# A two-layer decode block on one core: the last MLP block written out on its own

## The chip, the cores and the metric

One core of a Trainium2 chip runs the whole kernel. TensorE (PE) multiplies matrices out of SBUF into PSUM, VectorE (DVE) and ScalarE (ACT) work on SBUF and PSUM, GpSimd (POOL) on SBUF, and SyncE (SP) issues the DMA transfers between HBM and SBUF. Each engine works through its own instructions in order; they are ordered against each other by semaphores. The metric is device time in microseconds (us), less is better. The kernel before takes 1168.49 us, the median of 3 runs (1168.44 to 1168.51).

## What is computed

Eight sequences decode one token each. Attention over a cache of 8192 positions (32 query heads, 8 key heads, 128 wide) and an MLP (512 to 1792 to 512, SiLU) alternate, twice, with the same weights and the same cache both times:

```python
def _layernorm(x, axis=-1, eps=1e-5):
    m = jnp.mean(x, axis=axis, keepdims=True)
    v = jnp.var(x, axis=axis, keepdims=True)
    return (x - m) / jnp.sqrt(v + eps)
...
    def _B_ref(x, w1, w2):
        h = jnp.einsum("bsd,df->bsf", x, w1)
        h = _silu(h)
        out = jnp.einsum("bsf,fd->bsd", h, w2)
        return out

    x = A_x
    x = x + _A_ref(_layernorm(x, axis=-1), A_k_cache, A_v_cache, A_wq, A_wo)
    x = x + _B_ref(_layernorm(x, axis=-1), B_w1, B_w2)
    x = x + _A_ref(_layernorm(x, axis=-1), A_k_cache, A_v_cache, A_wq, A_wo)
    x = x + _B_ref(_layernorm(x, axis=-1), B_w1, B_w2)
    return x
```

x is (8, 1, 512) in bf16; the two caches have 128 MiB each. `_A_ref` is x@wq, softmax of the scaled scores, times V, and @wo.

## The kernel before, in words

**Tasks and steps.** A task is one attention over one (layer, sequence, key head): 2 x 8 x 8 = 128 tasks, in the order that `make_tasks` gives, and 8 steps to a task, so 1024 steps (NG). The main loop runs over the steps, p, and at each emits what is due there: key transposes (`emit_t_until`, VectorE, L487), scores (`emit_s`, TensorE, L553), the softmax of the task before in its phases (row maximum at phase 0, L564 and L566, then a GpSimd all-reduce, shift, exp on ScalarE at L580, and so on), P times V 14 steps behind the scores (`emit_pv`, L617), a copy and a fold of the result (L629, L634; the fold is a pair of fp32 matmuls), its scaling into the transposed activations (L646), and a head's part of the wo product (`add_heads`, L751). What is emitted earlier stands earlier in the queue of its engine.

**Loads.** Keys and values come in granules of 512 KB into the 28 slots of one SBUF area, `ARENA`. `plan_loads` sorts them by the step that needs them, picks a slot for each and notes the step behind which it may be issued; `issue_until(p)` issues those that are due, all on SyncE's queue. Part of the keys stays in its slots from the first layer to the second (`wide` loads). In the plan the last 28 loads go to 28 different slots: the first of them is the third granule of keys of sequence 7, head 0, into slot 20, which the scores of step 1005 read; the last is a granule of values.

**Ordering.** `op` and `mm_group` name what they read and write; `Sync.acquire` turns that into semaphore waits, leaves out what the engine has waited for already, and for TensorE leaves out waits on itself. VectorE and ScalarE do wait for their own earlier results.

**The last block.** Behind the loop the remaining heads are added up, and `block_stages` (L774) with n = 8 does residual, LayerNorm, MLP and residual for all eight sequences, the activations lying transposed as [128, 4, 8] (feature in the partition, four groups of 128, sequence). The same function with n = 1 does the first layer's block for one sequence at a time, inside the main loop. For n = 8:
- the residual: one VectorE add from the PSUM bank `MISC` (L763);
- `ln_stages` (L649): a reduce over the four groups (L686), an all-reduce over the partitions on GpSimd (L688), subtract (L694), square on ScalarE (L700), reduce (L701), all-reduce (L703), then the inverse root on VectorE, from a bit-shift seed by three Newton rounds (L708 to L718), and the product into `xnT` (L720). With n = 1 it goes by Ln and Exp on ScalarE instead (L669, L671) and one correcting step;
- w1: 56 matmuls into `MISC` (`project`, L733); SiLU as exp of the negative on ScalarE (L783), add 1, reciprocal, multiply on VectorE (L787 to L789), over 112 columns;
- w2: 56 matmuls into `MISC` (L733); the second residual (L763);
- four identity matmuls back to [8, 512] (L933), one VectorE copy to SBUF as bf16 (L940), one store (L942).

`SCp` are the two PSUM banks of the scores, `QSp` that of the expanded queries, `E` an fp32 SBUF tile which `P` and `Xr` view as bf16.

Of the kernel before, what the change touches and what calls it, by code (L numbers as in the profile page):

```python
# [8 lines left out]
LN_EPS = 1e-5  # L9
# [3 lines left out]
GUESS = 0.5 ** (1.0 / 3.0)  # L13

GRP = 8
GPT = 8
GPG = 2
NSLOT = 28
# [9 lines left out]
NSCP = 2  # L28
# [11 lines left out]
NAT = 2  # L40
CW = 32
SETTLE = 1

BF16 = mybir.dt.bfloat16
# [194 lines left out]
def _build(ctx, nc, A_x, A_k_cache, A_v_cache, A_wq, A_wo, B_w1, B_w2, out):  # L239
    B, _sq, D = A_x.shape  # L240
# [36 lines left out]
    ARENA = sb([128, NSLOT * SLOT], BF16, "arena")  # L277
# [67 lines left out]
    syn = Sync(nc, ctx)  # L345
# [6 lines left out]
    def res(name):  # L352
        if name not in R:
            R[name] = Res(name)
        return R[name]

    def r_half(slot, h):
        return res(f"slot{slot}_{h}")

    def op(eng, inst_fn, reads=(), writes=()):  # L360
        reads = [res(n) if isinstance(n, str) else n for n in reads]
        writes = [res(n) if isinstance(n, str) else n for n in writes]
        syn.acquire(eng, reads, writes)
        inst = inst_fn()
        tok = syn.mark(inst, eng)
        syn.release(tok, reads, writes)
        return tok
# [38 lines left out]
    with nc.Block() as block:  # L406

        @block.sync
        def _(sync_eng):
# [9 lines left out]
                reads=["ident"], writes=["ident"],  # L419
# [6 lines left out]
                reads=["ident"], writes=["hm"],  # L426
# [5 lines left out]
                reads=["ident"], writes=["own_x"],  # L432
# [3 lines left out]
            for n in range(NSCP):  # L436
# [11 lines left out]
               reads=["own_x", "hm"], writes=["sel"])  # L448
# [322 lines left out]

            settle = [idle] * SETTLE

            def block_stages(xs, rxs, n, fine=False):  # L774

                x0, x1, x2 = xs
                r0, r1, r2 = rxs
                p1, p2 = PIECES[:2] if fine else (1, 1)

                ev, re = (tiny["eh"], "eh") if n == 1 else (E[:, 0:FT * n], "P")  # L780

                def expo():
                    op(act, lambda: act.activation(ev, MISC[:, 0:FT * n], ACT.Exp, scale=-1.0),  # L783
                       reads=["MISC"], writes=[re])

                def silu():
                    op(dve, lambda: dve.tensor_scalar(ev, ev, 1.0, None, op0=ALU.add), reads=[re], writes=[re])  # L787
                    op(dve, lambda: dve.reciprocal(ev, ev), reads=[re], writes=[re])
                    op(dve, lambda: dve.tensor_tensor(hsT[:, 0:FT * n], MISC[:, 0:FT * n], ev, ALU.mult),  # L789
                       reads=["MISC", re], writes=["hsT"])  # L790

                def attended():
                    add_residual(x1, r1, x0, r0, n, CW if n == 1 else n)

                st = along([attended], ln_stages(x1, r1, n)) + settle
                st += joined(project(w1_sb, "w1", FT, KT, lambda k: xnT[:, k, 0:n], "xnT", n, p1), expo)
                st += [silu, idle]
                return st + joined(
                    project(w2_sb, "w2", KT, FT, lambda k: hsT[:, k * n:(k + 1) * n], "hsT", n, p2),
                    lambda: add_residual(x2, r2, x1, r1, n, n))  # L800

            def along(stages, more):
                return stages[:-1] + joined(stages[-1:], more[0]) + more[1:]
# [29 lines left out]
            def add_heads(b):  # L833
# [6 lines left out]
                else:  # L840
# [6 lines left out]
                        start=True, stop=True,  # L847
# [15 lines left out]

            emit_q(0)

            chain = []
            chain_b = [None]
            turn = [0]
# [11 lines left out]
            for p in range(NG + LP + GPT + FOLD + 1):  # L880
                tq = (p + LQ) // GPT
                if (p + LQ) % GPT == 0 and tq < ntask:
                    layer, b, _g = tasks[tq]
                    if layer == 1 and chain and chain_b[0] == b:
                        while chain:
                            chain.pop(0)()
                    emit_q(tq)
                emit_t_until(p + LT)
                if p % GPG == GPG - 1 and p < NG:
                    emit_s(p)  # L890
                if (p - LP) % GPG == GPG - 1 and 0 <= p - LP < NG:
                    emit_pv(p - LP)
                copied = p - LP - GPT
                if copied >= 0 and copied % GPT == 0 and copied // GPT < ntask:
                    emit_own(copied // GPT)
                folded = p - LP - GPT - FOLD_AT
                if folded >= 0 and folded % GPT == 0 and folded // GPT < ntask:
                    emit_fold(folded // GPT)
                ti, ph = p // GPT - 1, p % GPT
                if 0 <= ti < ntask and ph in soft:  # L900
                    for f in soft[ph]:
                        f(ti)
                if chain:
# [27 lines left out]
            mm_group(  # L931
                [
                    lambda kt=kt: pe.matmul(  # L933
                        MISC[0:B, kt * 128:(kt + 1) * 128], XT[0][:, kt, :], ident[:, :], start=True, stop=True,
                    )
                    for kt in range(KT)
                ],
                reads=["XT0", "ident"], writes=["MISC"],
            )
            op(dve, lambda: dve.tensor_copy(Xr[0:B, :], MISC[0:B, :]), reads=["MISC"], writes=["P"])  # L940
            syn.acquire(sp, reads=[res("P")])
            sp.dma_start(out_v, Xr[0:B, :]).then_inc(osem, 16)  # L942
            sp.wait_ge(osem, 16)

# [27 lines left out]
```

## Time and profile before

| | |
|---|---|
| median of 3 runs | 1168.49 us |
| the profiled execution | 1168.66 us |
| its span, first to last instruction | 1166.9 us |
| PE busy | 745.6 us (64%) |
| DVE busy | 628.2 us (54%) |
| ACT busy | 322.1 us (28%) |
| POOL busy | 117.9 us (10%) |
| moved by DMA | 467.10 MB, mean 400 GB/s |
| last transfer of values landed | 1150.6 us |
| last block's first residual starts | 1153.61 us |
| store issued | 1165.22 us |

Times in a profile run from the start of the span. A page has the busy share of each engine in 40 equal slices (a digit is tenths), the clock that TensorE was granted (PEclk, tenths), the chain of waits that ended last, and groups of instructions: line, engine, operation, output<-inputs, shape and count, then busy us and mean ns of one, then the engine's idle time ahead of them and what ended it. The timeline lists instructions as start, length, instruction, and in brackets the idle time of that engine before it and what it waited for. PEld is TensorE's weight load, which overlaps PE.

### The profile page before, as it was taken

The numbers are of one execution on the slowest core, as the hardware profiler recorded it, in microseconds if no ns is written. First come the engines' busy times: TensorE is split into PE (matmuls) and PEld (weight loads), VectorE is DVE, ScalarE is ACT, GpSimd is POOL, SyncE is SP. The second block draws the span as 40 slices with busy tenths as digits, with TensorE's granted clock in tenths as the row PEclk, the third lists the DMA queues.
The fourth block names the chain that finished last, engine by engine and source line by source line (L and its number), as shares of the span: only waits on it lengthen the run. The fifth ranks groups of instructions, "written<-read, shape, count | busy, mean of one in ns | idle before, by whom it ended". The sixth has DMA issues, their size and how long they took to land.

```text
span 1166.9 us, 31181 instructions
## 1 busy us (share of the span) xinstructions
PE 745.6 (64%) x13304; PEld 409.7 (35%) x13304; DVE 628.2 (54%) x1403; ACT 322.1 (28%) x756; POOL 117.9 (10%) x298
## 2 busy tenths in 40 slices
PE   1436676666756686567756676568766675567775
PEld 1213343234422353234423343235323442234333
DVE  3726662666446653656356553666266644566362
ACT  0202224223322224222413233223422233223331
POOL 0000011001100111001100110001100010001100
PEclk9755567655765568555765586655765577557755
DMA  9999999999999999999999999999999999999993
GB/s 363 395 396 411 408 403 412 417 410 402 403 418 413 408 391 414 415 409 407 407 415 411 403 393 415 416 408 407 410 417 409 400 398 420 411 408 407 408 408 143
DMA packets 116587, 467.10 MB, mean 400 GB/s; under 512 B 12240, under 2 KB 18144, under 8 KB 108768
## 3 DMA queue, kind: packets, MB, share of 16 engines
q1 hardware_dynamic: 116448, 465.11, 99.6%
q8 instruction: 104, 1.70, 0.6%
q14 instruction: 35, 0.29, 0.1%
HBM read 465.05 MB, written 0.01 MB: 399 GB/s over the span
## 4 chain that ended last, share of the span: by engine, by line
DMA 58%; SPq 22%; PE 12%; issue 4%; DVE 2%; ACT 0%; POOL 0%; POOLq 0%; DVEq 0%; ACTq 0%
DMA arena<-in_A_v_cache_dram 50%; SPq L374 22%; DMA arena<-in_A_k_cache_dram 8%; PE OTp L617 4%; PE SCp L553 3%; PE MISC L733 3%; PE OTp L634 2%; DVE arena L487 1%; PE TPp L598 1%; DVE row L564 0%; SPq L100 0%; PE MISC L751 0%; PE QSp L514 0%; POOL tops L569 0%; POOL ssa L589 0%
## 5 line engine op out<-in xcount | busy, mean ns | idle before, releaser
L487 DVE STREAM_TRANSPOSE arena<-arena 128x1024 int32<-128x1024 int32 x352 | 435.8, 1239 | 276.1 <-DMA arena<-in_A_k_cache_dram 276.0
L617 PE MATMUL OTp<-arena,PT 128*8 128x256 bf16 x4096 | 276.4, 365 | 364.5 <-DMA arena<-in_A_v_cache_dram 350.9
L580 ACT ACTIVATE E<-SCp,row 128x512 bf16<-128x512 f32 x128 | 181.1, 1415 | 489.0 <-DVE row L576 414.3
L553 PE MATMUL SCp<-arena,QB 128*16 128x128 bf16 (+2 forms) x4608 | 243.3, 354 | 11.1 <-DVE row L609 2.8
L617 PEld LDWEIGHTS OTp<-arena,PT 128*8 128x8 bf16 x4096 | 63.1, 86 | 509.3 <-DMA arena<-in_A_v_cache_dram 487.0
L553 PEld LDWEIGHTS SCp<-arena,QB 128*16 128x16 bf16 x4608 | 103.8, 108 | 69.6 <-issue 30.9
L634 PEld LDWEIGHTS OTp<-sel,E 128*128 128x128 f32 x512 | 103.6, 283 | 44.8 <-issue 32.8
L602 ACT COPY PT<-TPp 128x256 bf16<-128x256 bf16 x128 | 47.7, 373 | 252.0 <-PE TPp L598 252.0
L634 PE MATMUL OTp<-sel,E 128*128 128x4 f32 x512 | 114.7, 329 | 1.3 <-issue 0.8
L569 POOL PARTITION_ALL_REDUCE tops<-top x128 | 47.7, 373 | 549.0 <-DVE top L566 543.5
L589 POOL PARTITION_ALL_REDUCE ssa<-ssm x128 | 56.1, 438 | 384.8 <-ACT ssm L587 384.8
L564 DVE TENSOR_REDUCE row<-SCp 128x1 f32<-128x512 f32 x128 | 84.9, 663 | 11.9 <-PE SCp L553 11.8
L598 PE MATMUL TPp<-ident,E 128*128 128x128 bf16 x512 | 69.4, 281 | 3.7 <-ACT E L580 3.6
L609 DVE RECIPROCAL row<-ssa 128x4 f32<-128x4 f32 x128 | 18.7, 146 | 75.1 <-POOL ssa L589 75.1
L598 PEld LDWEIGHTS TPp<-ident,E 128*128 128x128 bf16 x512 | 39.3, 120 | 51.3 <-issue 31.6
L629 ACT COPY E<-OTp 128x256 f32<-128x256 f32 x128 | 48.2, 376 | 3.8 <-PE OTp L617 3.8
L733 PE MATMUL MISC<-xnT,wq 128*128 128x32 bf16 (+1 forms) x1152 | 35.6, 185 | 15.4 <-DVE xnT L720 14.3
L733 PEld LDWEIGHTS MISC<-xnT,wq 128*128 128x128 bf16 x1152 | 34.2, 104 | 21.9 <-issue 21.0
L751 PEld LDWEIGHTS MISC<-at,wo 128*128 128x128 bf16 x1024 | 33.1, 106 | 22.4 <-DVE row L576 10.1
L527 DVE TENSOR_TENSOR QB<-QSp,row 128x64 bf16<-128x64 f32 x128 | 25.8, 202 | 25.4 <-PE QSp L514 25.3
L587 ACT ACTIVATE ssm<-row 128x4 f32<-128x4 f32 x128 | 37.9, 296 | 3.9
L751 PE MATMUL MISC<-at,wo 128*128 128x32 bf16 x1024 | 37.5, 188 | 1.0 <-DVE row L573 0.4
(72 smaller groups left out, 278.9 us busy)
## 6 DMA issues: line engine op xcount, KB each, us to landing
arena<-in_A_v_cache_dram SPq DMA_DIRECT2D x512, 512.0 KB, 11.0
arena<-in_A_k_cache_dram SPq DMA_DIRECT2D x192, 512.0 KB, 8.2
arena<-in_A_k_cache_dram SPq DMA_DIRECT2D x24, 2048.0 KB, 22.4
arena<-in_A_k_cache_dram SPq DMA_DIRECT2D x32, 1024.0 KB, 20.3
wq<-in_A_wq_dram SPq DMA_DIRECT2D x1, 4096.0 KB, 16.3
wo<-in_A_wo_dram SPq DMA_DIRECT2D x1, 4096.0 KB, 34.7
w<-in_B_w_dram SPq DMA_DIRECT2D x2, 1792.0 KB, 27.1
E<-in_A_x_dram SPq DMA_DIRECT2D x1, 8.0 KB
```

The lines of the kernel that those rows point to most:

```text
L374: eng.dma_start(out_ap, in_ap).then_inc(counter.sem, 16)
L487: op(dve, lambda: dve.transpose(words, words), reads=[r_half(slot, 0), r_half(slot, 1)], writes=[r_half(slot, 0), r_half(slot, 1)])
L553: lambda n=n, t=t: pe.matmul(SCp[bank][t * QUAD:t * QUAD + USED, lo * 128:(lo + len(slots)) * 128], QB[qn][:, n, :], keys(t, n), start=(n ...
L564: op(dve, lambda: dve.tensor_reduce(rowmax[:, :], SCp[bank][:, :], AX.X, ALU.max), reads=[f"SC{bank}"], writes=["rowmax"])
L580: op(act, lambda: act.activation(P[:, :].rearrange("p (x j k) -> p k x j", x=CPB, k=NGRAN), SCp[bank][:, :].rearrange("p (k x j) -> p k x ...
L589: op(pool, lambda: pool.partition_all_reduce(ssa[st][:, :], ssm[st][:, :], 128, bass.bass_isa.ReduceOp.add), reads=[f"ssm{st}"], writes=[f ...
L598: lambda c=c: pe.transpose(tpv[:, c, :], P[:, c * 128:(c + 1) * 128], ident[:, :])
L617: lambda t=t, y=y: pe.matmul(OTp[ob][t * QUAD:t * QUAD + XW * REP, 0:XW * DH], PT[pb][:, k, t, y * XW:(y + 1) * XW].rearrange("p x r -> p ...
L629: op(act, lambda: act.copy(E[:, :], OTp[ob][:, 0:XW * DH]), reads=[f"OT{ob}"], writes=["P"])
L634: lambda x=x: pe.matmul(OTp[ob][:, 0:REP], E[:, x * DH:(x + 1) * DH], sel[:, x, :], start=(x == 0), stop=(x == XW - 1))
L733: lambda o=o, k=k: pe.matmul(MISC[:, o * n:o * n + w], w_sb[:, k, o * 128:(o + 1) * 128], rhs_of(k).to_broadcast([128, w]) if n == 1 else ...
L751: lambda o=o, h=h: pe.matmul(MISC[:, o * w:(o + 1) * w], wo_sb[:, h, o * 128:(o + 1) * 128], rhs_of(h).to_broadcast([128, w]) if n == 1 el ...
```

## The change

The last block no longer goes through `block_stages`. A function of its own, `last_block`, replaces it and what followed; `block_stages` with n = 1 and the main loop stay, but for one call.
- `last_constants`, called at the end of step NG - GPT = 1016, fills two 128x128 matrices with 1/512, one bf16 and one fp32, in the slot whose last load comes first in the plan. That slot's remaining space takes the block's small fp32 tiles.
- LayerNorm: four bf16 matmuls against the first matrix leave the mean of each sequence in every partition of `QSp`; VectorE subtracts, squares and reduces over the groups; one fp32 matmul against the second matrix leaves the variance. ScalarE takes Ln and Exp(-0.5 ...) with the constants of the n = 1 path, and VectorE one correcting round in three steps.
- The MLP in two halves of 7 x 128 hidden features. w1 of each half goes into its own bank of `SCp`; exp, add, reciprocal and multiply follow per half on 56 columns; w2 runs the first half's hidden features for all outputs and then the second's, adding up in `MISC`.
- The result: two identity matmuls into each bank of `SCp`, one half copied out by VectorE, the other by ScalarE; the store waits for both.

```diff
+            calm_slot = min(range(NSLOT), key=lambda n: max(d.slot <= n < d.slot + d.wide and i for i, d in enumerate(loads)))
+            r_calm = [r_half(calm_slot, h) for h in range(2)]
+            spare = ARENA[:, calm_slot * SLOT:(calm_slot + 1) * SLOT]
...
+            def last_constants():
+                op(dve, lambda: dve.memset(mean_w, 1.0 / D), writes=r_calm + ["mean_w"])
+                op(dve, lambda: dve.memset(var_w, 1.0 / D), reads=r_calm, writes=["var_w"])
+
+            def last_block():
...
+                mm_group([
+                    lambda k=k: pe.matmul(QSp[:, 0:B], mean_w, x1[:, k, :], start=(k == 0), stop=(k == KT - 1))
+                    for k in range(KT)
+                ], reads=["mean_w", "XT1"], writes=["QS"])
...
+                op(dve, lambda: dve.tensor_tensor(
+                    c3, x1[:, :, :], QSp[:, 0:B].unsqueeze(1).to_broadcast(wide), ALU.subtract),
+                   reads=["XT1", "QS"], writes=["c32"])
+                op(dve, lambda: dve.tensor_tensor(q32, c32, c32, ALU.mult), reads=["c32"], writes=["q32"])
+                op(dve, lambda: dve.tensor_reduce(part, q3.rearrange("p k b -> p b k"), AX.X, ALU.add),
+                   reads=["q32"], writes=["part"])
+                mm_group([lambda: pe.matmul(QSp[:, B:2 * B], var_w, part, start=True, stop=True)],
+                         reads=["var_w", "part"], writes=["QS"])
+                var = QSp[:, B:2 * B]
+                op(act, lambda: act.activation(gain, var, ACT.Ln, bias=eps[:, 0:1], scale=GUESS ** -2),
+                   reads=["QS", "eps"], writes=["gain"])
+                op(act, lambda: act.activation(gain, gain, ACT.Exp, scale=-0.5), reads=["gain"], writes=["gain"])
+                op(dve, lambda: dve.tensor_tensor(step_, gain, gain, ALU.mult), reads=["gain"], writes=["step_"])
+                op(dve, lambda: dve.scalar_tensor_tensor(step_, var, LN_EPS, step_, op0=ALU.add, op1=ALU.mult),
+                   reads=["QS", "step_"], writes=["step_"])
+                op(dve, lambda: dve.scalar_tensor_tensor(gain, step_, 3.0 * GUESS ** 2, gain, op0=ALU.subtract, op1=ALU.mult, reverse0=True),
+                   reads=["step_", "gain"], writes=["gain"])
+                op(dve, lambda: dve.tensor_tensor(xnT[:, :, :], c3, gain.unsqueeze(1).to_broadcast(wide), ALU.mult),
+                   reads=["c32", "gain"], writes=["xnT"])
...
+                for j, (lo, hi) in enumerate(zip(cut, cut[1:])):
+                    n = (hi - lo) * B
+                    bank, rb = SCp[j % NSCP], f"SC{j % NSCP}"
+                    mm_group([
+                        lambda o=o, k=k: pe.matmul(bank[:, (o - lo) * B:(o - lo + 1) * B], w1_sb[:, k, o * 128:(o + 1) * 128], xnT[:, k, :],
+                                                   start=(k == 0), stop=(k == KT - 1))
+                        for o in range(lo, hi) for k in range(KT)
+                    ], reads=["w1", "xnT"], writes=[rb])
+                    ev, re = E[:, lo * B:hi * B], f"e_{j}"
+                    op(act, lambda: act.activation(ev, bank[:, 0:n], ACT.Exp, scale=-1.0), reads=[rb, "P"], writes=[re])
+                    op(dve, lambda: dve.tensor_scalar(ev, ev, 1.0, None, op0=ALU.add), reads=[re], writes=[re])
+                    op(dve, lambda: dve.reciprocal(ev, ev), reads=[re], writes=[re])
+                    op(dve, lambda: dve.tensor_tensor(hsT[:, lo * B:hi * B], bank[:, 0:n], ev, ALU.mult),
+                       reads=[rb, re], writes=[f"hs_{j}"])
+                for j, (lo, hi) in enumerate(zip(cut, cut[1:])):
+                    mm_group([
+                        lambda o=o, k=k: pe.matmul(
+                            MISC[:, o * B:(o + 1) * B], w2_sb[:, k, o * 128:(o + 1) * 128], hsT[:, k * B:(k + 1) * B],
+                            start=(k == 0 and o == 0), stop=(k == FT - 1), skip_group_check=True)
+                        for k in range(lo, hi) for o in range(KT)
+                    ], reads=["w2", f"hs_{j}"], writes=["MISC"])
...
+                op(dve, lambda: dve.tensor_copy(Xr[0:B, 0:w], SCp[0][0:B, 0:w]),
+                   reads=["SC0"] + [f"e_{j}" for j in range(HALVES)], writes=["P"])
+                op(act, lambda: act.copy(Xr[0:B, w:D], SCp[1][0:B, 0:w]),
+                   reads=["SC1"] + [f"e_{j}" for j in range(HALVES)], writes=["P2"])
...
                 issue_until(p)
+                if p == NG - GPT:
+                    last_constants()
...
-            for f in block_stages([XT[2][:, :, :], XT[1][:, :, :], XT[0][:, :, :]], ["XT2", "XT1", "XT0"], B):
-                f()
...
-            op(dve, lambda: dve.tensor_copy(Xr[0:B, :], MISC[0:B, :]), reads=["MISC"], writes=["P"])
-            syn.acquire(sp, reads=[res("P")])
+            last_block()
+            syn.acquire(sp, reads=[res("P"), res("P2")])
             sp.dma_start(out_v, Xr[0:B, :]).then_inc(osem, 16)
             sp.wait_ge(osem, 16)
```

More of the change, by code (lines that the diff above doesn't have):

```diff
@@ L42 @@
 SETTLE = 1
+HALVES = 2
 BF16 = mybir.dt.bfloat16
@@ L864, in _ @@
             emit_q(0)
+            calm_slot = min(range(NSLOT), key=lambda n: max(d.slot <= n < d.slot + d.wide and i for i, d in enumerate(loads)))
+            r_calm = [r_half(calm_slot, h) for h in range(2)]
+            spare = ARENA[:, calm_slot * SLOT:(calm_slot + 1) * SLOT]
+            mean_w = spare[:, 0:128]
+            words = spare[:, 128:].bitcast(FP32)
+            var_w, c32, q32 = words[:, 0:128], words[:, 128:128 + KT * B], words[:, 160:160 + KT * B]
+            part, gain, step_ = words[:, 192:192 + B], words[:, 200:200 + B], words[:, 208:208 + B]
@@ new lines, in last_constants @@
+            def last_constants():
+                op(dve, lambda: dve.memset(mean_w, 1.0 / D), writes=r_calm + ["mean_w"])
+                op(dve, lambda: dve.memset(var_w, 1.0 / D), reads=r_calm, writes=["var_w"])
+            def last_block():
+                x0, x1, x2 = XT[2], XT[1], XT[0]
+                op(dve, lambda: dve.tensor_tensor(
+                    x1[:, :, :], MISC[:, 0:KT * B].rearrange("p (k b) -> p k b", b=B), x0[:, :, :], ALU.add),
+                   reads=["MISC", "XT2"], writes=["XT1"])
+                mm_group([
+                    lambda k=k: pe.matmul(QSp[:, 0:B], mean_w, x1[:, k, :], start=(k == 0), stop=(k == KT - 1))
+                    for k in range(KT)
+                ], reads=["mean_w", "XT1"], writes=["QS"])
+                wide = [128, KT, B]
+                c3, q3 = c32.rearrange("p (k b) -> p k b", b=B), q32.rearrange("p (k b) -> p k b", b=B)
+                op(dve, lambda: dve.tensor_tensor(
+                    c3, x1[:, :, :], QSp[:, 0:B].unsqueeze(1).to_broadcast(wide), ALU.subtract),
[16 more added lines that the diff above has]
+                   reads=["c32", "gain"], writes=["xnT"])
+                cut = [FT * j // HALVES for j in range(HALVES + 1)]
+                for j, (lo, hi) in enumerate(zip(cut, cut[1:])):
[19 more added lines that the diff above has]
+                    ], reads=["w2", f"hs_{j}"], writes=["MISC"])
+                op(dve, lambda: dve.tensor_tensor(
+                    x2[:, :, :], MISC[:, 0:KT * B].rearrange("p (k b) -> p k b", b=B), x1[:, :, :], ALU.add),
+                   reads=["MISC", "XT1"], writes=["XT0"])
+                w = D // 2
+                for j in range(2):
+                    mm_group([
+                        lambda k=k: pe.matmul(SCp[j][0:B, (k - j * KT // 2) * 128:(k - j * KT // 2 + 1) * 128], x2[:, k, :],
+                                              ident[:, :], start=True, stop=True)
+                        for k in range(j * KT // 2, (j + 1) * KT // 2)
+                    ], reads=["XT0", "ident"], writes=[f"SC{j}"])
+                op(dve, lambda: dve.tensor_copy(Xr[0:B, 0:w], SCp[0][0:B, 0:w]),
+                   reads=["SC0"] + [f"e_{j}" for j in range(HALVES)], writes=["P"])
+                op(act, lambda: act.copy(Xr[0:B, w:D], SCp[1][0:B, 0:w]),
+                   reads=["SC1"] + [f"e_{j}" for j in range(HALVES)], writes=["P2"])
@@ L928, in _ @@
             assert summed == [HKV] * (B + 1)
-            for f in block_stages([XT[2][:, :, :], XT[1][:, :, :], XT[0][:, :, :]], ["XT2", "XT1", "XT0"], B):
-                f()
[L931 to L940, printed above, removed]
-            syn.acquire(sp, reads=[res("P")])
+            last_block()
+            syn.acquire(sp, reads=[res("P"), res("P2")])
             sp.dma_start(out_v, Xr[0:B, :]).then_inc(osem, 16)
```

## The prediction, made before the changed kernel was run

> **What bounds the kernel now.** I read the page first (its slices and the chain of waits), then the stretches of the last 70 us, then the tail instruction by instruction in the timeline, and last the groups of instructions by form, for durations.
>
> ```profile
> span 1166.9 us, 31181 instructions
> PEclk9755567655765568555765586655765577557755
> DMA  9999999999999999999999999999999999999993
> ...
> DMA 58%; SPq 22%; PE 12%; issue 4%; DVE 2%; ACT 0%; POOL 0%; POOLq 0%; DVEq 0%; ACTq 0%
> ```
>
> The DMA engines are full in 39 of 40 slices and the chain is 58% DMA and 22% SyncE's queue, which issues those transfers. So nothing ahead of the last transfer matters unless it delays a load. The tail behind it is another matter, as the stretches show (columns: busy us and count on PE, weight load, DVE, ACT, POOL; granted clock; DMA share; GB/s):
>
> ```profile
> 1140.00:1150.00 10.00, 8.59 (x124) 4.77 (x128) 2.18 (x9) 3.02 (x7) 0.80 (x2) 0.50 0.81 324
> 1150.00:1153.60 3.60, 2.68 (x36) 1.54 (x28) 0.16 (x1) 0.37 (x1) 0.00 (x0) 0.50 0.00 1
> 1153.60:1158.40 4.80, 0.00 (x0) 0.00 (x0) 2.99 (x17) 0.18 (x1) 0.82 (x2) 0.50 0.00 2
> ```
>
> The transfers end at 1150.6. From 1153.6 one engine at a time works, so every us cut there comes off the end one for one. That tail in the timeline (start, length, instruction):
>
> ```profile
> 1153.61 0.19 DVE L763 TENSOR_TENSOR XT<-MISC,XT 128x32 bf16<-128x32 f32 x1 [0.69 <-PE MISC L751]
> ...
> 1158.17 0.19 DVE L720 TENSOR_TENSOR xnT<-MISC,row 128x32 bf16<-128x32 f32 x1
> ...
> 1158.42 1.65 PE L733 MATMUL MISC<-xnT,w 128*128 128x8 bf16 x56 [4.85 <-DVE xnT L720]
> 1160.11 0.26 ACT L783 ACTIVATE E<-MISC 128x112 f32<-128x112 f32 x1 [5.12 <-PE MISC L733]
> 1160.41 0.22 DVE L787 TENSOR_SCALAR E<-E 128x112 f32<-128x112 f32 x1 [2.04 <-ACT E L783]
> 1160.66 0.85 DVE L788 RECIPROCAL E<-E 128x112 f32<-128x112 f32 x1
> 1161.62 0.28 DVE L789 TENSOR_TENSOR hsT<-MISC,E 128x112 bf16<-128x112 f32 x1
> ...
> 1161.95 1.66 PE L733 MATMUL MISC<-hsT,w 128*128 128x8 bf16 x56 [1.88 <-DVE hsT L789]
> ...
> 1163.89 0.59 PE L933 MATMUL MISC<-ident,XT 128*8 128x128 bf16 x4 [0.28 <-DVE XT L763]
> 1164.52 0.68 DVE L940 CAST E<-MISC 8x512 bf16<-8x512 f32 x1 [0.68 <-PE MISC L933]
> 1165.22 0.31 SPq L942 DMA_DIRECT2D out_dram<-E  x1
> ```
>
> Handovers read off these rows: DVE to PE 0.06 (1158.36 to 1158.42), PE to DVE 0.03, PE to ACT 0.04, ACT to DVE 0.04, a DVE step to a dependent DVE step 0.03 (so a 0.17 step has a pitch of 0.20), but 0.10 behind the reciprocal (1161.51 to 1161.62).
>
> **Step 1, the constants.** Two VectorE memsets of 128x128 come at the end of step 1016, behind the row maximum of the last task but one. The rows have 128x512 f32 at 485 ns and 128x1 at 59, so 128 elements are about 59 + 127 x 0.83 = 165 ns, 0.33 us for both. VectorE finishes L566 at 1133.72 and then sits idle for 0.43 until the next key transpose at 1134.15, whose keys are still in flight; the memsets fit. If they did not, the next transposes have 1.00 and 1.28 us of idle before them, so 2.7 us of cover in all; beyond that, the keys of the last task are late, then its softmax, then the last P·V, which today waits only 0.16 for its values, and the end moves one for one. The wait is met: by the load plan the slot picked is 20, last filled with keys (batch 7, group 0) that the scores of step 1005 read, and the row maximum of step 1016, earlier in VectorE's own queue, has waited for scores of step 1015. SyncE has no load left for that slot. Cost: nothing.
>
> **Step 2, LayerNorm**, from the end of the residual (1153.80) to the first w1 matmul (1158.42): 4.62 us, all of it replaced. New chain:
> - 0.06, then four matmuls on 8 columns: the four of L845 took 0.24, sixteen of L751 0.60; I take 0.26, near the row with the same count.
> - 0.03, subtract 0.19 (L763: the same shape, PSUM and SBUF in); 0.03, square 0.19; 0.03, reduce 0.19 (L701).
> - 0.06, one fp32 matmul on 128 fp32 columns of weights. The fold L634 does two such, as four records, in 1.01 at the tail's clock of 0.50 and in 0.61 at 1065 us at a higher one. Bounds 0.30 and 1.01; one is a pitch of 0.22 and a latency of 0.35, 0.57, since the clock stays at 0.50.
> - 0.04, Ln: 0.30 (L669, with the same bias column) though 0.18 was enough for a square out of PSUM (L700); I take 0.30. 0.04, Exp 0.20 (L671). The shapes are 128x8 instead of 128x1, which the 128x14 and 128x112 of L783 (183 and 264 ns) price at 0.01.
> - 0.04, three dependent VectorE steps at the 0.20 pitch of L715 to L718, 0.60, then xnT 0.19, then 0.06.
>
> Sum 0.32 + 0.66 + 0.63 + 0.58 + 0.89 = 3.08. **Gain 1.54.** Little of it is the reductions: reduce to next VectorE step took 0.54 across GpSimd (1154.04 to 1154.58) and takes 0.35 and 0.67 across PE. It is the eleven seed and Newton steps, 2.2 us, becoming two ScalarE steps and three VectorE steps, and one reduce less.
>
> The rows that the two ScalarE steps rest on, with the table:
>
> ```profile
> L669 ACT ACTIVATE row<-s2a,row 128x1 f32<-128x1 f32 x16 | 4.7, 296 | 4.2 <-POOL s2a L662 4.2
> ...
> L671 ACT ACTIVATE row<-row 128x1 f32<-128x1 f32 x16 | 3.2, 203 | 0.5
> ...
> L450 ACT ACT_TABLE_LOAD x1 | 1.3, 1283 | 0.8 <-PEq L957 0.8
> ```
>
> Ln, Exp, Square and Copy alternate through the whole program on one table load. [...]
>
> **Step 3, the MLP in halves.** Today 5.18 us from the first w1 matmul to the last w2 matmul (1158.42 to 1163.60). New, from the first w1 matmul: 28 matmuls end at 0.168 + 27 x 0.027 = 0.90 (56 took 1.65). 0.04, exp on 56 columns 0.22 (between 183 ns at 14 and 264 at 112); 0.04; add 0.19; 0.03; reciprocal at 56: rows 146 ns at 4, 242 at 14, 853 at 112, so 6.2 ns an element, 0.50; 0.10; multiply 0.22 (172 and 276). First half done at 2.24. The second half's matmuls end at 1.65 and its exp at 1.91, before VectorE is free: hidden under the first half's reciprocal. VectorE is the bound: 0.03 + 1.04 more, 3.31. The first half of w2 (2.30 to 3.20) hides under that. Then 0.05 and 28 matmuls, 0.90: 4.26. **Gain 0.92**: the two halves of w1 and w2 that are now covered are worth 1.65, and VectorE pays most of a second set of fixed costs.
>
> **Step 4, the output.** Today from the identity matmuls (1163.89) to the issue (1165.22) 1.33. New: all four end at 0.59; ScalarE copies 256 columns in 0.37 (L629, 128x256, 376 ns), issue at 0.59 + 0.04 + 0.37 + 0.03 = 1.03. VectorE's half starts at 0.43 and takes some 0.4 (half of 0.68 and a fixed part), done at 0.84, hidden. SyncE's second wait delays nothing; its queue holds only the store. The store itself is unchanged. **Gain 0.29.**
>
> **Sum:** 1.54 + 0.92 + 0.29 = 2.75. The span goes from 1166.9 to 1164.15. The profiled execution took 1168.66, 1.76 around its span; the median of the runs is 1168.49, so I forecast 1165.7. Bounds: mean matmuls 0.24 to 0.36, fp32 matmul 0.30 to 1.01, Ln 0.18 to 0.30, each reciprocal 0.45 to 0.60, unlisted handovers 0.02 either way at fifteen places. Not all go wrong together: gain 2.2 to 3.3.
>
> **Rivals.**
> - *The fp32 matmul is the new wait.* One isolated fp32 matmul, behind an idle PE at half clock, costs as much as the fold's pair: 1.01 instead of 0.57. For it: PE has no neighbour instruction to overlap its weight load with, and the fold's pair does. Against: 354 ns median of one record. Gain 2.3, time 1166.2.
> - *Halving buys nothing on VectorE.* The reciprocal takes 0.85 at 56 columns as at 112: second half done at 4.0, w2 at 4.95, gain 2.06, time 1166.4. Against it stand 146, 242 and 853 ns at 4, 14 and 112.
> - *ScalarE switches tables* for Ln and again for Exp: two loads of 1.28, gain 0.2, time 1168.3. Against: one load today. [...]
> - *Slower: the stream of loads runs slower in the new program.* Place: the 1149 us of transfers, at 400 GB/s, with slices between 391 and 420 behind the first. Decides from a loss of 0.24% of rate (2.75 of 1149), which cancels the gain; a loss of 0.5%, 398 GB/s, would cost 5.7 and give 1171.4. Against: every instruction up to 1133.7 is the same, the loads and their order too, and the three runs lie within 0.07 us.
>
> **How the numbers follow.** 0.2%, about what a measurement of this kernel can tell from no change, is 2.34 us: 1166.15 is the edge of "faster", 1170.8 that of "slower". The sum as worked: 0.75. The fp32 wait 0.11, the reciprocal 0.06, the table 0.03, the stream 0.05. Of the sum's own spread (2.2 to 3.3) perhaps a twentieth lies under 2.34; the fp32 rival sits on the edge and I count two thirds of it as "same", with all of the reciprocal and most of the table. Stream shifts that are smaller than the rival's go to "same". Faster 0.75, same 0.20, slower 0.05. The range reaches from 3.5 gained to 1.7 gained, 1165.0 to 1166.8, and takes in the first two rivals.
>
> **What would show it.** The residual still starts at 1153.6 and two memsets stand at 1133.7 with no later transpose moved (step 1). The first w1 matmul at 1156.9 (step 2): if later, look at the length of the fp32 matmul and of Ln. The last w2 matmul 4.26 behind the first w1 matmul, with two reciprocals near 0.50 and no VectorE idle between the halves (step 3). The store issued 1.03 behind the first identity matmul (step 4). One table load. The forecast is wrong if the residual of the last block starts more than half a us away from 1153.6, or if one link of the new chain is over 0.4 us longer than its row.

## The result, and the profile after

| | before | changed |
|---|---|---|
| median of 22 runs each | 1168.62 us | 1166.38 us |
| ratio, 95% interval | | 0.9982, 0.9976 to 0.9987 |
| the profiled execution | 1168.66 us | 1166.42 us |
| its span | 1166.94 us | 1164.27 us |
| time around the span, mean | 1.73 us (92 runs beside the experiments) | 2.15 us (these 22 runs) |
| last block's first residual starts | 1153.61 us | 1153.60 us |
| store issued | 1165.22 us | 1162.54 us |
| store behind that residual | 11.61 us | 8.94 us |

Faster by 2.24 us (interval 1.5 to 2.8); 2.75 was forecast (1165.7), and the range of 1165.0 to 1166.8 holds the time. The page of the changed kernel, its span, load slices and chain:

```profile
span 1164.3 us, 31191 instructions
...
DMA  9999999999999999999999999999999999999994
...
DMA 59%; SPq 23%; PE 13%; issue 3%; DVE 1%; ACT 0%; DVEq 0%; ACTq 0%
```

The stream of loads bounds the kernel as before, and in these two profiles the last block starts at the same time. What was gained is the tail's, in the timeline of the changed kernel (start, length, instruction, idle time of that engine before it):

```profile
1133.68 0.17 DVE L876 MEMSET arena<- 128x128 bf16 x1
...
1133.94 0.17 DVE L877 MEMSET arena<- 128x128 f32 x1
1134.14 1.25 DVE L488 STREAM_TRANSPOSE arena<-arena 128x1024 int32<-128x1024 int32 x1
...
1153.60 0.19 DVE L882 TENSOR_TENSOR XT<-MISC,XT 128x32 bf16<-128x32 f32 x1 [0.69 <-PE MISC L752]
...
1153.85 0.27 PE L886 MATMUL QSp<-XT,arena 128*128 128x8 bf16 x4 [0.29 <-DVE XT L882]
1154.22 0.19 DVE L891 TENSOR_TENSOR arena<-XT,QSp 128x32 f32<-128x32 bf16 x1 [0.43 <-PE QSp L886]
...
1154.93 0.60 PE L897 MATMUL QSp<-arena 128*128 128x8 f32 x2 [0.81 <-DVE arena L895]
1155.57 0.27 ACT L900 ACTIVATE arena<-QSp,row 128x8 f32<-128x8 f32 x1 [3.92 <-PE QSp L897]
1155.87 0.21 ACT L902 ACTIVATE arena<-arena 128x8 f32<-128x8 f32 x1
1156.11 0.17 DVE L903 TENSOR_TENSOR arena<-arena 128x8 f32<-128x8 f32 x1 [1.23 <-ACT arena L902]
1156.38 0.17 DVE L904 SCALAR_TENSOR_TENSOR arena<-QSp,arena 128x8 f32<-128x8 f32 x1
...
1157.03 1.65 PE L916 MATMUL SCp<-xnT,w 128*128 128x8 bf16 x56 [1.50 <-DVE xnT L908]
...
1158.45 0.50 DVE L923 RECIPROCAL E<-E 128x56 f32<-128x56 f32 x1
...
1159.06 0.22 DVE L924 TENSOR_TENSOR hsT<-SCp,E 128x56 bf16<-128x56 f32 x1
...
1159.33 1.87 PE L928 MATMUL MISC<-hsT,w 128*128 128x8 bf16 x56 [0.65 <-DVE hsT L924]
...
1161.48 0.59 PE L939 MATMUL SCp<-ident,XT 128*8 128x128 bf16 x4 [0.28 <-DVE XT L933]
...
1162.11 0.36 ACT L945 CAST E<-SCp 8x256 bf16<-8x256 f32 x1 [3.17 <-PE SCp L939]
1162.54 0.31 SPq L1015 DMA_DIRECT2D out_dram<-E  x1
```

The memsets end just ahead of a transpose that starts where it did (1134.15 before). LayerNorm takes 3.24 us from the end of the residual (1153.79) to the first w1 matmul, against 4.62. The first w1 to the last w2 matmul takes 4.17 (1157.03 to 1161.20), against 5.18; both halves of w2 are merged in the row of 56. The first identity matmul (1161.48) to the store takes 1.06, against 1.33. That makes 2.66, and 2.67 from residual to store, while the runs gained 2.24. The medians alone can't tell these apart (1.5 to 2.8). But the time around the span, which no timeline shows, grew by 0.42: it is 1.68 to 1.81 in every run of the kernel before and 2.11 to 2.26 in every run of the changed one. Two things therefore needed runs: whether the parts are worth what the links say, and what grew outside the span.

### The profile page after: what moved, and what is told of

Its sections match the earlier page's. It is cut to its first block, busy times and chain, and to the rows that moved or that the text cites. A ratio compares the mean times of both kernels' runs of the same rounds, so it can differ in the third digit from the quotient of the medians.

```text
span 1164.3 us, 31191 instructions
## 1 busy us (share of the span) xinstructions
PE 746.6 (64%) x13310; PEld 410.3 (35%) x13310; DVE 627.4 (54%) x1399; ACT 323.1 (28%) x759; POOL 116.8 (10%) x296
## 4 chain that ended last, share of the span: by engine, by line
DMA 59%; SPq 23%; PE 13%; issue 3%; DVE 1%; ACT 0%; DVEq 0%; ACTq 0%
DMA arena<-in_A_v_cache_dram 52%; SPq L375 22%; DMA arena<-in_A_k_cache_dram 7%; PE OTp L618 5%; PE MISC L734 3%; PE SCp L554 3%; PE OTp L635 2%; DVE arena L488 1%; PE TPp L599 0%; PE MISC L752 0%; SPq L101 0%; PE QSp L515 0%; ACT QT L819 0%; DVE QB L528 0%; DVE E L923 0%
## 5 line engine op out<-in xcount | busy, mean ns | idle before, releaser
L635 PEld LDWEIGHTS OTp<-sel,E 128*128 128x128 f32 x512 | 101.0, 277 | 44.3 <-issue 32.6
L635 PE MATMUL OTp<-sel,E 128*128 128x4 f32 x512 | 112.2, 324 | 1.1 <-issue 0.7
```

The lines of the kernel that those rows point to most:

```text
L635: lambda x=x: pe.matmul(OTp[ob][:, 0:REP], E[:, x * DH:(x + 1) * DH], sel[:, x, :], start=(x == 0), stop=(x == XW - 1))
```

## The experiments

Each starts from the changed kernel. In the table "tail" is the store's start less the start of the last block's first residual in the profiled execution, "around" the mean time of the runs outside their span (1.73 on the mean of the 92 runs of the kernel before beside them), "runs" the median time, with the ratio to the kernel before beside it.

| run | tail | around | runs | ratio, interval |
|---|---|---|---|---|
| e1 old LayerNorm | 10.31 | 1.72 | 1167.67 | 0.9989 (0.9980 to 0.9998) |
| e2 MLP in one piece | 9.96 | 2.15 | 1167.57 | 0.9988 (0.9979 to 0.9997) |
| e3 old output | 9.21 | 2.18 | 1166.74 | 0.9982 (0.9973 to 0.9990) |
| e4 memsets behind the residual | 9.00 | 2.16 | 1166.50 | 0.9979 (0.9970 to 0.9988) |
| e5 one GpSimd all-reduce more | 8.93 | 1.80 | 1166.45 | 0.9980 (0.9971 to 0.9988) |
| e6 second waits moved | 8.81 | 2.18 | 1166.47 | 0.9981 (0.9972 to 0.9989) |
| e7 variance by bf16 matmuls | 8.37 | 2.15 | 1166.08 | 0.9977 (0.9968 to 0.9986) |
| e8 second part's SiLU on ScalarE | 8.66 | 2.18 | 1166.41 | 0.9979 (0.9970 to 0.9988) |
| e9 four GpSimd memsets at the start | 8.93 | 1.75 | 1166.52 | 0.9980 (0.9971 to 0.9989) |
| e10 second waits dropped | 8.65 | 2.18 | 1166.08 | 0.9977 (0.9967 to 0.9986) |
| e11 all that gained (6 runs) | 7.88 | 1.75 | 1164.96 | 0.9967 (0.9956 to 0.9979) |
| e12 the changed kernel again | 8.93 | 2.18 | 1166.48 | 0.9978 (0.9969 to 0.9987) |

Among these profiles the residual itself starts anywhere from 1153.40 to 1154.51, and in the changed kernel alone at 1153.60 and 1154.09. So store times and spans of two profiles can't be compared to better than half a us to one us; medians of 11 runs scatter by some 0.3. The tail is the same to 0.01 in the two profiles of the changed kernel. I read sizes from the tail; the medians confirm only the larger ones.

**e1, LayerNorm as before.**

```diff
-                mm_group([
-                    lambda k=k: pe.matmul(QSp[:, 0:B], mean_w, x1[:, k, :], start=(k == 0), stop=(k == KT - 1))
...
-                op(dve, lambda: dve.tensor_tensor(xnT[:, :, :], c3, gain.unsqueeze(1).to_broadcast(wide), ALU.mult),
-                   reads=["c32", "gain"], writes=["xnT"])
+                for f in ln_stages(x1[:, :, :], "XT1", B):
+                    f()
...
-                if p == NG - GPT:
-                    last_constants()
```

> The changed kernel with LayerNorm as before (GpSimd all-reduces, seed and three Newton rounds) and without the two memsets; halves and split output stay. Theory A, the tail is one chain and each part is worth the difference of its links: from the end of the residual to the first w1 matmul 4.62 us again instead of 3.24, the store issued at 1163.9 instead of 1162.54, span 1165.7, time 1.4 over the changed kernel's, about 1167.8. Theory B, part of what the tail gains is lost outside the span (the time around the span was 1.76 us before and is 2.1 in every run of the changed kernel): if LayerNorm's new ScalarE or TensorE steps are the part that causes it, the time around the span falls back to 1.76 here and the kernel is only 1.0 over the changed one.

The tail grew by 1.37, as theory A has it, and the time around the span fell to 1.72, as theory B has it. Both hold as far as the sizes go: LayerNorm is worth 1.37 in the chain and gives 0.43 of it back outside the span. Which of its parts does that, e1 doesn't say. Against the kernel before beside them, the runs gain 1.09 where the changed kernel gains 2.24: 1.15 less instead of the 0.94 that this leaves, within their scatter.

**e2, the MLP in one piece.**

```diff
-HALVES = 2
+HALVES = 1
```

> The changed kernel with the MLP in one piece of 112 columns in one PSUM bank; the rest stays. Theory A: first w1 matmul to last w2 matmul 5.18 us instead of 4.18, reciprocal 0.85, the store at 1163.5, span 1165.3, time 1.0 over the changed kernel's. A rival to A, that the halves hide no more than VectorE's second set of fixed costs gives back, has the store within 0.3 of 1162.5. Theory B: around the span 1.76 if the second bank's use is the cause, else 2.1.

Tail 1.02 longer, the runs 1.05 (a gain of 1.19 instead of 2.24). The rival falls, and with 2.15 around the span the halves aren't what grew there. In its timeline one reciprocal of 0.85 stands between w1 and w2, and TensorE idles 1.88:

```profile
1159.40 0.85 DVE L923 RECIPROCAL E<-E 128x112 f32<-128x112 f32 x1
...
1160.70 1.66 PE L928 MATMUL MISC<-hsT,w 128*128 128x8 bf16 x56 [1.88 <-DVE hsT L924]
```

**e3, one copy of the result.**

```diff
-                op(dve, lambda: dve.tensor_copy(Xr[0:B, 0:w], SCp[0][0:B, 0:w]),
...
-                op(act, lambda: act.copy(Xr[0:B, w:D], SCp[1][0:B, 0:w]),
+                op(dve, lambda: dve.tensor_copy(Xr[0:B, :], MISC[0:B, :]),
```

> The changed kernel with one VectorE copy of all 512 columns from one bank instead of two copies by two engines; the rest stays. Theory A: first identity matmul to store 1.33 us instead of 1.06, span 1164.6, time 0.27 over the changed kernel's. Theory B, with ScalarE's late copy as the part that costs 0.36 outside the span: around the span 1.76 and the time 0.1 under the changed kernel's.

Tail 0.27 longer, around the span no change: the output's gain is as costed and ScalarE's late copy isn't what costs time behind the span.

**e4, the memsets without cover.**

```diff
-                if p == NG - GPT:
-                    last_constants()
...
                    reads=["MISC", "XT2"], writes=["XT1"])
+                last_constants()
```

> The changed kernel with the two memsets taken out of the loop and put directly behind the last block's residual, where nothing covers them. Theory A, the memsets cost nothing only because VectorE waits for keys there: the first is now ahead of the mean's matmuls, 0.2 us, the second runs beside them; the store 0.2 to 0.4 later, at 1162.7 to 1162.9. The rival, that in the loop they cost something after all (a later transpose, SyncE's waits that name the memset), has the residual start earlier than 1153.6 here and the store no later than 1162.5.

Only 0.06 longer, less than the 0.2 to 0.4 expected, though the mean's matmuls start 0.14 later behind the residual. The rival falls too: the residual starts at 1153.63. The timeline of e4 says why:

```profile
1153.63 0.19 DVE L882 TENSOR_TENSOR XT<-MISC,XT 128x32 bf16<-128x32 f32 x1 [0.69 <-PE MISC L752]
1153.79 0.17 DVE L876 MEMSET arena<- 128x128 bf16 x1
...
1154.02 0.27 PE L887 MATMUL QSp<-XT,arena 128*128 128x8 bf16 x4 [0.43 <-DVE arena L876]
1154.05 0.17 DVE L877 MEMSET arena<- 128x128 f32 x1
1154.32 0.19 DVE L892 TENSOR_TENSOR arena<-XT,QSp 128x32 f32<-128x32 bf16 x1
```

The matmuls end at 1154.29 and the subtract starts 0.03 later. In the changed kernel they end at 1154.12 and it starts 0.10 later. The difference: there the subtract waits for TensorE and for VectorE's own residual; here the second memset has waited for the first, which stands behind the residual in VectorE's queue, so that no wait for the residual is left. That became theory C, in e6 and e10.

**e5 and e9, what grew behind the span.**

```diff
+                op(pool, lambda: pool.partition_all_reduce(s1a[:, 0:B], s1[:, 0:B], 128, bass.bass_isa.ReduceOp.add),
+                   reads=["XT1", "s1"], writes=["s1a"])
```

> The changed kernel with one GpSimd all-reduce added beside the last block, started by its first residual; nothing reads its result and it is on no chain. The time around the span was 1.75 us in every run of the kernel before and of the changed kernel with the old LayerNorm, and 2.14 in every run of the others, so something in the new LayerNorm makes it 0.39 longer. Theory B1, GpSimd: it has no work in the last 16 us of the changed kernel and had some up to 10 us before the end in the other two; then this run has 1.75 around the span, the same span, and a time of about 1166.0. The rival, that it lies in what the new steps add on TensorE, ScalarE or VectorE or in the length of a program: still 2.14 and no change of the time.

The time around the span fell to 1.80 but the time did not: the span's end came later behind the same store (2.02 instead of 1.73). In SyncE's own waits (who is waited for, us in total, times, longest), the last barrier, first of the changed kernel, then of e5:

```profile
SPq L407 <- PEq L407: 0.2, 1, 0.2
```

```profile
SPq L407 <- PEq L407: 0.5, 1, 0.5
```

Behind that line the trace has GpSimd's two last semaphore steps 0.375 us apart instead of 0.08. So 0.3 of a stall had moved into view, and idleness was not its cause. e9 adds four instructions at the other end of GpSimd's program:

```diff
+            for _n in range(4):
+                op(pool, lambda: pool.memset(s1a[:, :], 0.0), writes=["s1a"])
```

> The changed kernel with four small GpSimd memsets added at its start, some 1150 us before the end; nothing else differs. In the run with one all-reduce more the 0.39 us did not go: 0.3 of it moved from behind the span into it, between GpSimd's two last semaphore steps (0.375 apart instead of 0.08), and the time stayed. Theory B2: GpSimd stalls some 0.36 at a fixed place in its program, counted in instructions, just behind its 452nd recorded one; the new LayerNorm has three records fewer there, so the stall fell from a place where GpSimd waits anyway onto its last steps, on which the end of the program waits. Then four more instructions anywhere put it back: around the span 1.75, the two last steps 0.08 apart, time 0.36 under the changed kernel's in this set. Theory B1, long idleness at the end: nothing at the start can change that, 2.15 as before.

Around the span 1.75, and the last steps 0.08 apart: four instructions 1150 us earlier took the stall out of the end. With the counts of GpSimd's records, 455 in the kernel before and in e1 (1.73, 1.72 around), 453 in e5 (stall between the last two), 452 in the changed kernel (stall behind the last), 457 in e9 (the four and one semaphore step), this fits a stall at a fixed place in GpSimd's program, behind its 452nd record: the change slid the last steps under it by leaving out two all-reduces and a wait. The traces show one more thing near that place. The instruction queue with packets of 8 KB, in the page of the kernel before, then of the changed one (packets inside the span, MB, share):

```profile
q14 instruction: 35, 0.29, 0.1%
```

```profile
q14 instruction: 34, 0.28, 0.1%
```

It has 35 in the four kernels without the stall at their end (before, e1, e9, e11) and 34 in all the others. In the trace the last packet starts at 1155.85 in the kernel before and at 1140.94 in e9, but at 1165.48 in the changed kernel, behind its span; in every profile that is behind GpSimd's 452nd or 453rd record. e9 edits GpSimd's program alone and moves it (1140.94 instead of 1165.48), so I take the packet to be GpSimd's. GpSimd doesn't wait for the packet itself: in e5 its last step, behind the stall, starts at 1164.51 and the packet at 1165.22. What it does in the stall, and what the packet has to do with it, isn't in the traces.

That e9 runs faster was not shown: 1166.52, beside 1166.48 for e12. Its tail and the 1.72 from store to end of span are those of the changed kernel, so its longer spans (median 1164.8, from 1163.9 to 1165.4) should come from ahead of the last block; the one profile is of a shorter run (1164.1). That the stall costs time is only suggested, by all the runs together: where it lies at the end, the gain of the median is on average 0.47 smaller than that of the tail (ten kernels, 0.24 to 0.72), and where it doesn't, 0.17 smaller (three, -0.11 to 0.40).

**e6 and e10, two waits on one step.** Both take the second wait off four VectorE steps, where the first implies it. e10 leaves it out; e6 leaves it out at the subtract and has an earlier step take it at the other three. The edit of e10, then what e6 adds to it (at L904 the wait is then left out because L903 has waited):

```diff
-                   reads=["XT1", "QS"], writes=["c32"])
+                   reads=["QS"], writes=["c32"])
...
-                   reads=["QS", "step_"], writes=["step_"])
+                   reads=["step_"], writes=["step_"])
...
-                       reads=[rb, re], writes=[f"hs_{j}"])
+                       reads=[re], writes=[f"hs_{j}"])
```

```diff
-                op(dve, lambda: dve.tensor_tensor(step_, gain, gain, ALU.mult), reads=["gain"], writes=["step_"])
+                op(dve, lambda: dve.tensor_tensor(step_, gain, gain, ALU.mult), reads=["QS", "gain"], writes=["step_"])
...
-                    op(dve, lambda: dve.tensor_scalar(ev, ev, 1.0, None, op0=ALU.add), reads=[re], writes=[re])
+                    op(dve, lambda: dve.tensor_scalar(ev, ev, 1.0, None, op0=ALU.add), reads=[rb, re], writes=[re])
```

> The changed kernel with the same instructions, but four VectorE steps that waited for two engines at once (the subtract, the second correcting step, the multiply of each half) now wait for one: the other wait is left out where the first implies it, or is put on an earlier step that stands idle anyway. Theory C: a VectorE step with two waits starts 0.10 us behind its input and one with a single wait 0.03, which is what the prediction's handovers left out; then these four gaps fall to 0.03 or 0.04, the store comes at 1162.3 and the time falls by 0.25. The rival, which is how the prediction explained the gap in the kernel before, that the 0.10 is the reciprocal's own tail: the gap ahead of the two multiplies stays 0.10 and the store moves by 0.13 at most.

> The changed kernel with the second wait dropped from four VectorE steps (subtract, second correcting step, the multiply of each half) where the first implies it, and put nowhere else. Theory C: 0.06 to 0.07 less at each, the store 8.67 behind the last block's first residual instead of 8.94, time 0.27 less. In the run that moved the waits, two of the four gaps came up again at the step that took the wait, and the store was 8.81 behind the residual. The rival, that these gaps belong to reading PSUM behind another step: no gain over 8.81.

e6 moved the tail by only 0.13, the size the rival named, but not in its way. Its timeline:

```profile
1156.22 0.21 ACT L902 ACTIVATE arena<-arena 128x8 f32<-128x8 f32 x1
1156.53 0.17 DVE L903 TENSOR_TENSOR arena<-arena 128x8 f32<-128x8 f32 x1 [1.30 <-ACT arena L902]
1156.73 0.17 DVE L904 SCALAR_TENSOR_TENSOR arena<-QSp,arena 128x8 f32<-128x8 f32 x1
...
1158.87 0.50 DVE L923 RECIPROCAL E<-E 128x56 f32<-128x56 f32 x1
...
1159.41 0.22 DVE L924 TENSOR_TENSOR hsT<-SCp,E 128x56 bf16<-128x56 f32 x1
```

Behind the reciprocal the gap is 0.04: it was not the reciprocal's tail. L904 now starts 0.03 behind L903, but L903, which took the wait, starts 0.10 behind ScalarE: here the second wait cost its time though it had been met 0.6 us before. What e6 gained are the subtract's 0.07 and that of the second multiply, whose add starts while VectorE is still busy. e10, which drops the waits, has a tail of 8.65, as expected from theory C (8.67). Its trace has 1538 VectorE records against 1542: the four semaphore steps of 0.02 that stood 0.065 ahead of those instructions are not there. The tail is 0.28 shorter than in e12, 0.07 for each of the four.

The chains also show the next bound. Of the changed kernel, then of e10 (start, us, what):

```profile
1160.02 0.23 DVE hsT L924
1160.24 0.05 issue
1160.29 0.92 PE MISC L928 x28
```

```profile
1158.64 0.23 DVE hsT L924
1158.87 0.05 issue
1158.91 1.81 PE MISC L928 x56
```

In e10 w2 is one piece of the chain, but its second half still waits a little. The row is 1.79 long, where it is 1.87 in the changed kernel and 1.66 in e2, which has no halves:

```profile
1158.91 1.79 PE L928 MATMUL MISC<-hsT,w 128*128 128x8 bf16 x56 [0.57 <-DVE hsT L924]
```

In the trace the starts of its matmuls lie 0.03 apart, and 0.14 between the halves (0.22 in the changed kernel). So TensorE is nearly the bound of w2, and some 0.12 of VectorE's time is left on the chain.

**e7, the variance in bf16**, an approximation of the squares that the changed kernel doesn't make:

```diff
+                q16 = spare[:, 1024:1024 + KT * B]
+                op(dve, lambda: dve.tensor_tensor(q16, c32, c32, ALU.mult), reads=["c32"], writes=["q32"])
+                mm_group([
+                    lambda k=k: pe.matmul(QSp[:, B:2 * B], mean_w, q16[:, k * B:(k + 1) * B], start=(k == 0), stop=(k == KT - 1))
...
-                op(dve, lambda: dve.tensor_reduce(part, q3.rearrange("p k b -> p b k"), AX.X, ALU.add),
...
-                mm_group([lambda: pe.matmul(QSp[:, B:2 * B], var_w, part, start=True, stop=True)],
```

> The changed kernel with the squares written as bf16 and the variance taken by four bf16 matmuls against the mean's matrix, so that the reduce over the groups and the fp32 matmul go, and the second memset too. Theory A, links by their records: 0.27 for four bf16 matmuls instead of 0.60 for the fp32 one, and 0.25 for the reduce and its handover gone; the store at 1161.95, span 1163.7, time 0.6 less. The rival, that an isolated TensorE hop costs its latency whatever it carries: the matmuls still take about 0.5 and the store comes at 1162.2.

Tail 0.57 shorter (8.37). The matmuls of e7, where the changed kernel's fp32 one takes 0.60:

```profile
1155.02 0.27 PE L896 MATMUL QSp<-arena 128*128 128x8 bf16 x4 [0.58 <-DVE arena L894]
```

**e8, the second part's SiLU on ScalarE.**

```diff
-                cut = [FT * j // HALVES for j in range(HALVES + 1)]
+                cut = [0, 6, FT]
...
+                    if j:
+                        op(act, lambda: act.activation(ev, ev, ACT.Ln, bias=1.0), reads=[re], writes=[re])
+                        op(act, lambda: act.activation(ev, ev, ACT.Exp, scale=-1.0), reads=[re], writes=[re])
+                    else:
```

> The changed kernel with the halves cut 6 to 8 and the second part's 1/(1+e) taken on ScalarE as exp(-ln(1+e)), the first part's left on VectorE. Theory A: VectorE's reciprocals in a row are what bounds the MLP (3.2 of 4.18 us), so with the two parts on two engines the first part is done 2.1 behind the first w1 matmul, the second at 2.8, and the last w2 matmul at 3.85 instead of 4.18; the store at 1162.2. The rival, that w2 on TensorE is the bound already: last w2 matmul within 0.1 of 4.18. If a table had to be loaded, a load of 1.28 us would show on ScalarE and the kernel would be over 1 us slower.

Tail 0.28 shorter; first w1 to last w2 matmul 3.89. No table was loaded: the trace has the one load at the start, as before. The edit moves the cut and the engine together, so the run doesn't say which of them gained, and the median (1166.41) doesn't show the gain.

**e11 and e12, all that gained, beside the changed kernel.** e11 joins the edits of e7, e8, e10 and e9.

> The changed kernel with all that gained: bf16 squares and no fp32 matmul, second part of the SiLU on ScalarE with the parts cut 6 to 8, no second waits, four GpSimd instructions at the start. If the gains add, 0.57 + 0.28 + 0.22 (the last half's wait is off the chain here): the store 7.9 behind the residual, around the span 1.75, time 1.4 under the changed kernel's in this set and 3.7 under the kernel before. If the parts get in each other's way on ScalarE, the store comes at 8.1 or more.

> The changed kernel itself, beside the other three on one chip. Store 8.94 behind the residual, around the span 2.15, and a time 2.25 under the kernel before: 2.68 by which the store comes earlier less some 0.4 behind the span.

e11: tail 7.88, around the span 1.75, 1164.96: 3.84 under the kernel before and 1.52 under the changed one, where 1.05 of tail and 0.42 around the span make 1.47. The gains added up, and its median is the lowest here. e12 repeats the changed kernel: 8.93 and 2.18.

## Why the prediction was right, and where it was off

- *Step 1, the constants for nothing:* right. Two rows of 0.17 inside the idle 0.43, the next transpose not moved (1134.14, 1134.15 before). The cover mattered less than feared: e4 puts them on the chain for 0.06, since 0.07 of their 0.14 comes back with the wait that they spare.
- *Step 2, LayerNorm 3.08:* 3.24 measured. The fp32 matmul took 0.60 against 0.57 and Ln 0.27 against 0.30, so the rival of an isolated fp32 matmul at 1.01 falls. What was missing is the handover: 0.03 was carried to the subtract and to the second correcting step, which wait twice and took 0.10 each (e6, e10).
- *Step 3, the MLP 4.26:* 4.17. The reciprocal at 0.50 is the interpolated one, and the second rival falls with e2. The 0.10 ahead of the multiply was the right size for the wrong reason: two waits, not the reciprocal. It came out shorter because the second half's add starts before the first half's multiply has ended.
- *Step 4, the output 1.03:* 1.06, ScalarE's copy 0.36. SyncE's second wait was said to delay nothing: the store starts 0.07 behind the last copy, against 0.03 in the kernel before and in e3, where it waits for one engine.
- *The sum of the links:* 2.67 instead of 2.75. It is that close partly by luck, since the errors of steps 2 to 4 (0.16 longer, 0.09 shorter, 0.03 longer) cancel in part.
- *The sum against the median:* this is the step that failed. The 1.76 around the span (1.73 with a span that isn't rounded) was carried over as a constant; it became 2.15. By e5 and e9 (1.80 and 1.75) it is GpSimd's program: it got shorter, from 455 records to 452, and its stall fell on the last barrier. 2.67 of chain less 0.42 is 2.25, beside the 2.24 measured; with an interval of 1.5 to 2.8, that close a fit is luck.
- *The chances:* 0.75 stood on a gain of over 2.34 us. The median gain of 2.24 lies just under it, where 0.20 stood, and the interval reaches to both sides.
- *The other rivals:* one table load, of 1.28, stands in the trace, and the stream's rate is unchanged (mean 401 GB/s against 400).

## What to carry to other kernels

This tail, in which one engine works at a time, could be costed link by link from rows of the same kernel, the four steps to 0.16 us or better, and what was missed was mostly the number of engines that a step waits for: naming one producer instead of two at four steps, where it implied the other, took 0.28 off the tail (e10). Such a gain is checked against the distance between two instructions of the tail, since the start of the last block lay anywhere from 1153.40 to 1154.51 in these profiles, a range wider than most of the single gains. And what lies outside the span differed from program to program (1.72 to 2.18 here): compare it before adding a span's gain to a median.

## What the runs showed of the hardware

At four VectorE steps a second wait cost 0.07 us each (0.10 behind the input instead of 0.03; e4, e6, e10), in e6 even where it had been met 0.6 us before. The store on SyncE started 0.07 behind ScalarE's copy where it waited for two engines (the changed kernel), and 0.03 behind VectorE's where it waited for one (the kernel before, e3); no run has it wait for ScalarE alone. The reciprocal took 0.45, 0.50 and 0.85 at 48, 56 and 112 columns (e8, the changed kernel, e2), 6.2 ns for each column more. GpSimd's last two steps lie 0.375 us apart in e5, on both sides of the place behind its 452nd record, and 0.08 in the changed kernel, whose program ends at that place; there the time around the span is 2.15, and 1.72 to 1.80 in e1, e5, e9 and e11, where GpSimd's program goes on. A stall of some 0.4 us at that place is what I read from these numbers. In two profiles of the changed kernel the last block starts 0.49 us apart.
